# Token factor of a norm as a ScalarE step, norm weights folded into the gate and value rows, and a new hand-written order for the first stage

## The chip, the cores and the metric

One Trainium2 chip, one core of it. The metric is the device time of one execution in microseconds (us). The engines that appear below are TensorE (PE in the rows; its weight loads are PEld), VectorE (DVE), ScalarE (ACT), GpSimd (POOL) and SyncE (SP), which here issues the DMA transfers. Each engine runs its own instructions in the order of the program and waits at the first one whose inputs or buffers are not ready.

## What is computed

Attention in chunks of 64 tokens, an RMS norm with a weight per column, a gated layer, and a second layer with a cosine gate:

```python
scores = scale * np.matmul(q_c, k_c.transpose(0, 1, 2, 4, 3))
scores = scores - np.max(scores, axis=-1, keepdims=True)
attn = np.exp(scores)
attn = attn / (np.sum(attn, axis=-1, keepdims=True) + 1e-09)
out = np.matmul(attn, v_c)
...
rms = np.sqrt(np.mean(x * x, axis=-1, keepdims=True) + 1e-06)
xn = x / rms * rms_g
g = xn @ w_gate
silu = g * (1.0 / (1.0 + np.exp(-g)))
val = xn @ w_val
x = silu * val @ w_out
...
h = x @ w_in
return (h * np.cos(h)) @ w_out2
```

There are 4608 tokens of 512 columns (8 heads of 64), d_ff is 1536 in the first layer and 2048 in the second, all in float32.

## The kernel before

**Stages.** Stage 1 does the attention and the norm of all tokens and, beside them, the first four of the twelve blocks of 128 gate and value columns ("plain" blocks f = 0 to 3). The later stages do the rest of the gate and value columns, and the other three products, by a seven-product scheme on halves of the matrices. Every float32 product is made of three matmuls on high and low parts (`mm3`, L293): high times high, high times low, low times high. The change lies in stage 1, and in weights that stage 1 prepares for the next stage.

**Stage 1.** The tokens are 36 units of 128, taken as 18 pairs, and their products run over chunks of tokens A to K: A to D have 256 tokens, E to K have 512. A step of stage 1 has a letter and a number, and the steps stand in one hand-written list, ORDER (L643 on), which is emitted as it stands; so each engine sees its own instructions in the order of that list. The steps that matter here:

- `Q`, `V`, `D`, `Dg`: loads of queries and keys, of values, of raw plain weights, and of the norm's weights. `Q0` is split in two halves. `Dg` loads `gamma` broadcast to 128x512.
- `s` (and `sx`, the second unit of the first pair): 64x64 score matmuls of a pair on PE (L404), into one PSUM bank for each unit. `m` (L417) row maxima and `b` (L425) subtraction on DVE, `e` (L429) exponential on ACT, `n` (L434 to L436) sum and reciprocal on DVE.
- the product p·z (L444): on GpSimd as a step `z` for units under POOL_Z, on DVE at the end of `n` for the others. `t` (L451) transposes of p on PE, `c` (L456) copy of them on ACT, `v` (L467) the value matmuls of a pair on PE, into `o`.
- the norm: `r` (L481) squares and sums on ACT, `w` (L486, L488) the token factor `rs` on GpSimd, `y` (L492) `xn = o * rs * gamma` on DVE, `x` (L500) transposes on PE into `tr`.
- operands: `j` (L509) cast of `tr` to the high part `xt` and `a` (L514) copy to `xf`, both on ACT; `l` the low part, on GpSimd (L520) for units under POOL_L, on DVE (L522) for the others.
- a plain weight fm (f the block, m = 0 gate, 1 value): `k` (L119, ACT), `p` (L122, L123, DVE) and `q` (L127, L128, DVE) round it, `H` (L544, ACT) casts the high part, `L` (L546, GpSimd) makes the low part.
- the sixteen weights of the later blocks, `P` steps with a number: `Pl` load, `Pa` (L119, ACT), `Pb` (L122, L123, DVE), `Pc` (L127, L128, DVE), `Pd` sums (L198, GpSimd), `Ph` casts (L610, ACT), `Po` low parts (L614, GpSimd), `Pk` store. In the rows they are the tile `wt`.
- `gCf`, `vCf`: the twelve gate or value matmuls of chunk C and block f on PE; `S` (L568) silu on ACT, `h` (L578) product on DVE, `Y` store.

PE runs `gA0` only when `w[0,0]` has its high and low part and the operands of units 0 and 1 stand; in the list the steps `v0`, `v2`, the scores of four pairs, six `t` and four `x` stand ahead of it. The silu of ACT and its exponential use different function tables, so a step `S` after an `e` (or the reverse) is preceded by a table load.

Of the kernel before, what the change touches and what calls it, by code (L numbers as in the profile page):

```python
# [40 lines left out]
POOL_Z = 4  # L41
POOL_L = 4
# [40 lines left out]
def kernel(  # L83
# [26 lines left out]
    def f32(a):  # L110
        return a.bitcast(F32)
# [247 lines left out]
    with ExitStack() as st:  # L359
# [4 lines left out]
        gamma = tp.tile([P, D], F32, tag="gamma", name="gamma")  # L364
# [24 lines left out]
        def part(h):  # L389
            return slice(h * HD, (h + 1) * HD)  # L390
# [4 lines left out]
        def att_s(u, which=(0, 1)):  # L395
            for b in which:
                at = ps_g.tile([P, D], F32, tag="gv", name="sc") if u // 2 in (1, 3) else bank("sc")
                unit[u + b]["sc"] = at.rearrange("p (a b) -> p a b", b=HD)
            for hp in range(NHP):
                for c in range(2):  # L400
                    for b in which:
# [56 lines left out]
        def att_v(u):  # L458
            for b in range(2):
                unit[u + b]["o"] = bank("o")  # L460
            for hp in range(NHP):
                for h in range(2):
                    for b in range(2):
                        s = unit[u + b]
                        for c in range(2):
# [3 lines left out]
                                s["pts"][part(c ^ b), hp, part(h ^ b)],  # L469
# [64 lines left out]
        def conv_step(kind, f, m):  # L534
            if kind == "k":
                conv[f, m] = wp.tile([P, D], U32, tag=f"p{8 + (2 * f + m) % 7}", name="t")
# [49 lines left out]
        def prep_step(kind, j):  # L586
# [34 lines left out]
        units.update({"s": lambda u: att_s(2 * u, (0, 1) if u else (0,)), "z": unit_z, "v": lambda u: att_v(2 * u), "W": lambda k: free(f"p{k}")})  # L621
        units["O"] = lambda j: (hig(0, j), log(0, j))

        def step(name):
            kind, n = name[0], name[1:]
            if name == "Dg":
                nc.sync.dma_start(out=gamma, in_=rms_g[None, :].to_broadcast([P, D]))
            elif name == "sx":
                att_s(0, (1,))
# [14 lines left out]
            Q0 s0 I m0 Q1 b0 sx Q2 e0 m1 Q3 b1 e1 V0 n0 D21 D20 z0 s1 n1 z1 t0 k21 m2 m3 b2 b3 p21 t1 c0 V1 Pl0 e2 c1 e3 n2  # L644
            z2 k20 Dg v0 r0 Q4 n3 q21 w0 p20 Pa0 r1 t2 w1 y0 z3 x0 Q5 c2 t3 H21 a0 j0 Pb0 y1 x1 V2 V3 D00 s2 q20 Q6 D01 c3
            j1 a1 H20 Pc0 m4 m5 b4 v1 b5 e4 r2 e5 L20 l1 r3 n4 n5 Q7 V4 t4 t5 w2 k01 w3 l0 V5 c4 y2 Pl1 k00 D10 p00 y3 x2 c5
            s3 q00 a2 j2 p01 x3 H00 a3 v2 m6 L21 q01 l2 L00 b6 X0 D11 r5 r4 m7 gA2 w4 y4 H01 gA0 vA2 b7 L01 k10 j3 e6 n6 Q8
            V6 x4 vA0 V7 Q9 Pl2 SA2 l3 w5 SA0 t6 e7 p10 hA2 y5 D30 Q10 n7 gB2 x5 D31 Q11 a4 j4 c6 a5 l4 j5 gB0 t7 c7 V8 l5
            hA0 s4 v3 SB2 k11 m8 q10 X1 Pa1 Pd0 m9 b8 H10 vB2 r6 SB0 vB0 w6 V9 r7 w7 hB2 hB0 p11 b9 y6 L10 gC0 gC2 x6 e8 q11
            vC2 e9 gC1 SC0 SC2 n8 vC0 y7 n9 k31 j6 gA1 hC2 H11 Ph0 L11 t9 Po0 hC0 l6 t8 k30 a6 SA1 s5 p30 YA2 Q12 c9 Q13 q30  # L650
            m10 YB2 SC1 x7 a7 p31 b10 YB0 YC0 V10 j7 c8 H30 q31 m11 vC1 YA0 e10 YC2 vA1 hC1 L30 b11 v4 gB1 hA1 l7 r9 e11 X2
            w9 SB1 r8 w8 n10 X3 n11 y8 gB3 H31 gA3 y9 t10 V11 vB1 YC1 SB3 Pa2 L31 t11 s6 Pb2 Pb1 m12 hB1 c10 SA3 vA3 b12 m13
            vB3 Pk0 c11 x8 e12 hA3 b13 x9 e13 v5 j8 a8 Pc1 n12 hB3 a9 gD1 r10 r11 j9 l8 n13 Pd1 w10 l9 V12 Q14 Q15 V13 gD0
            w11 vD1 gD3 t13 y11 YA3 SD1 c13 hD1 y10 t12 s7 x10 Pc2 c12 vD0 m15 m14 Q16 Ph1 Pl3 V14 x11 Po1 j10 SD0 gC3 V15
            Q17 SD3 a10 b14 l10 b15 e14 e15 hD0 j11 v6 r13 a11 SC3 r12 Pa3 w13 Pd2 YB1 Q18 w12 n15 l11 n14 vD3 vC3 Pk1 y13
            YA1 Ph2 hC3 t15 gD2 V16 X4 Pl4 y12 t14 vD2 c14 Po2 s8 Pb3 hD3 c15 x12 SD2 V17 Q19 j12 Pa4 a12 m16 b16 hD2 m17
# [677 lines left out]
```

## Time and profile before

| | us |
|---|---|
| median of 3 runs | 1636.64 |
| lowest, highest | 1635.1, 1636.64 |
| profiled execution, its own time | 1635.3 |
| its span | 1633.5 |
| PE busy in the span | 1604.3 (98%) |
| DVE, ACT, POOL busy in the span | 1378.7, 959.5, 243.2 |

The profile is of one execution. A window's row gives the busy time of each engine in a stretch; a timeline lists instructions with their start and length, runs of like ones on one line; a waits view names for an engine what ended each of its waits; the chain is the work that ended last, followed back from the end; lines by form group equal instructions and give the mean of one in ns.

### The profile page before, as it was taken

How to read it: one execution, taken by the hardware profiler on the slowest of the kernel's cores; microseconds unless marked ns; L12 is line 12 of the kernel's file. 1: busy time of each engine (PE TensorE's matmuls, PEld its weight loads, DVE VectorE, ACT ScalarE, POOL GpSimd, SP SyncE). 2: the span in 40 equal slices, each digit the busy share in tenths (PEclk: the TensorE clock that was granted, in tenths of full speed). 3: DMA queues.
4: the chain of work that ended last, by engine and by line, in shares of the span. 5: the costliest groups of instructions: out<-in, count | busy, mean ns of one | idle time of the engine just before them, and what ended most of it. 6: DMA issues, size and time to landing. Idle time of an engine off the chain costs nothing.

```text
span 1633.5 us, 29216 instructions
## 1 busy us (share of the span) xinstructions
PE 1604.3 (98%) x11208; PEld 1556.4 (95%) x11208; DVE 1378.7 (84%) x1854; ACT 959.5 (59%) x1380; POOL 243.2 (15%) x280
## 2 busy tenths in 40 slices
PE   5999999999999999999999999999999999999998
PEld 4988888999999999999999999999999999999998
DVE  7988785589998997899999788988989977877885
ACT  4877665344555654455554578888888644434443
POOL 4434353023322222001112000000000000000000
PEclk7999999999999999999999999999999999999999
DMA  9588987898678679877576974434433665346331
GB/s 316 198 264 287 302 267 253 288 309 275 200 241 263 219 217 294 322 235 226 187 227 216 335 264 136 155 121 141 138 124 119 235 211 160 101 126 184 108 100 35
DMA packets 293531, 342.98 MB, mean 210 GB/s; under 512 B 87952, under 2 KB 266128, under 8 KB 293392
## 3 DMA queue, kind: packets, MB, share of 16 engines
q1 hardware_dynamic: 292592, 341.02, 64.4%
q8 instruction: 88, 1.44, 0.3%
q14 instruction: 51, 0.42, 0.1%
q10 hardware_dynamic: 800, 0.10, 0.0%
HBM read 197.92 MB, written 143.13 MB: 209 GB/s over the span
## 4 chain that ended last, share of the span: by engine, by line
PE 88%; DVE 6%; DMA 3%; issue 1%; ACT 1%; SPq 1%; POOL 0%; DVEq 0%; ACTq 0%; POOLq 0%
PE b L293 74%; PE v L293 6%; PE g L293 5%; DMA kout<-wout 1%; PE sc L404 1%; PE tr L500 1%; PE o L467 1%; DMA qk<-in_qk_dram 1%; PE pt L451 1%; DVE z L793 0%; DMA w<-kgv 0%; DVE z L782 0%; DVE xo L840 0%; DVE wraw L198 0%; DVE wt L127 0%
## 5 line engine op out<-in xcount | busy, mean ns | idle before, releaser
L293 PE MATMUL b<-xo,w 128*128 128x384 f32 x3528 | 613.0, 334 | 0.3 <-DVE xo L840 0.3
L293 PEld LDWEIGHTS b<-xo,w 128*128 128x128 f32 x3528 | 611.4, 188 | 1.6 <-ACT xo L280 0.7
L293 PE MATMUL b<-xt,w 128*128 128x384 f32 x1728 | 305.2, 335 | 2.3 <-ACT z L778 1.4
L293 PEld LDWEIGHTS b<-xt,w 128*128 128x128 f32 x1728 | 299.6, 188 | 4.5 <-ACT z L778 2.9
L293 PE MATMUL b<-x,w 128*128 128x384 f32 x1440 | 262.3, 335 | 1.4 <-DVE z L782 1.4
L293 PEld LDWEIGHTS b<-x,w 128*128 128x128 f32 x1440 | 250.1, 188 | 3.1 <-DVE z L782 2.0
L280 ACT CAST xo<-q 128x768 fp32r<-128x768 f32 x144 | 118.3, 836 | 117.6 <-PE b L293 97.7
L281 DVE TENSOR_TENSOR xo<-q,xo 128x768 fp32r<-128x768 f32 x144 | 135.3, 954 | 53.2 <-ACT xo L280 53.0
L293 PE MATMUL b<-q,w 128*128 128x384 f32 x864 | 158.0, 334 | 0.0
L293 PEld LDWEIGHTS b<-q,w 128*128 128x128 f32 x864 | 150.5, 188 | 0.2 <-DVE q L945 0.2
L835 ACT CAST xo<-rawh 128x768 fp32r<-128x768 f32 x98 | 80.0, 836 | 62.3 <-PE b L293 41.4
L251 POOL TENSOR_TENSOR wout<-wt,wout 128x384 fp32r<-128x384 f32 x44 | 51.4, 1169 | 424.9 <-ACT wout L249 329.5
L778 ACT COPY z<-b 128x768 f32<-128x768 f32 x72 | 57.6, 800 | 86.7 <-PE b L293 66.1
L293 PE MATMUL v<-xt,w 128*128 128x512 f32 (+1 forms) x528 | 108.2, 356 | 0.0
L293 PE MATMUL g<-xt,w 128*128 128x512 f32 (+1 forms) x528 | 107.6, 356 | 0.0
L840 DVE TENSOR_TENSOR xo<-rawh,xo 128x768 fp32r<-128x768 f32 x98 | 96.9, 1021 | 7.1 <-ACT xo L835 7.0
L293 PEld LDWEIGHTS g<-xt,w 128*128 128x128 f32 x528 | 85.4, 189 | 13.2
L293 PEld LDWEIGHTS v<-xt,w 128*128 128x128 f32 x528 | 85.4, 189 | 12.9
L782 DVE TENSOR_TENSOR z<-b,z 128x768 f32<-128x768 f32 x72 | 68.6, 953 | 29.8 <-PE b L293 22.2
L923 DVE TENSOR_TENSOR u<-b,z 128x768 f32<-128x768 f32 x72 | 68.6, 953 | 17.1 <-ACT z L918 14.0
L251 POOL TENSOR_TENSOR wout<-wraw,wout 128x512 fp32r<-128x512 f32 x44 | 69.5, 1581 | 71.3 <-ACT wout L249 67.0
L943 DVE SCALAR_TENSOR_TENSOR q<-q,u 128x768 f32<-128x768 f32 x72 | 68.5, 953 | 12.1 <-ACT q L941 11.7
(134 smaller groups left out, 2099.8 us busy)
## 6 DMA issues: line engine op xcount, KB each, us to landing
wraw<-in_w_dram SPq DMA_DIRECT2D x240, 128.0 KB, 3.6
gd<-q SPq DMA_DIRECT2D x80, 384.0 KB, 2.5
q<-gd SPq DMA_DIRECT2D x80, 384.0 KB, 4.0
rawh<-hd SPq DMA_DIRECT2D x66, 384.0 KB, 4.8
w<-kout SPq DMA_DIRECT2D x49, 512.0 KB, 6.3
qk<-in_qk_dram SPq DMA_DIRECT2D x35, 512.0 KB, 6.1
kgv<-wout SPq DMA_DIRECT2D x16, 896.0 KB, 5.9
w<-kgv SPq DMA_DIRECT2D x28, 512.0 KB, 6.3
```

Of the source, the lines that this page charges most:

```text
L251: nc.gpsimd.tensor_tensor(b[n][:, :, 1], a, f32(b[n][:, :, 0]), op=ALU.subtract)
L280: nc.scalar.copy(hi, a)
L281: nc.vector.tensor_tensor(lo, a, f32(hi), op=ALU.subtract)
L293: nc.tensor.matmul(acc, a, b, start=first and k == 0 and q == 0, stop=k == n - 1 and q == 2, skip_group_check=True)
L404: nc.tensor.matmul(sc[part(h ^ b), 2 * hp + (c ^ b), :], t[part(h), 0, hp, part(c)], t[part(h), 1, hp, part(c)], start=True, stop=True,)
L451: nc.tensor.transpose(s["pt"][:, hp, :], p[:, 2 * hp : 2 * hp + 2, :].rearrange("p a b -> p (a b)"), ident)
L778: nc.scalar.copy(sums[s, g, k], z[s, g, "b1"])
L782: nc.vector.tensor_tensor(t, z[s, g, "b2" if k == 0 else "b5"], t, op=ALU.add)
L835: nc.scalar.copy(to[0], source2(s, g, j))
L840: nc.vector.tensor_tensor(to[1], source2(s, g, j), f32(to[0]), op=ALU.subtract)
L923: nc.vector.tensor_tensor(t, acc, part, op=ALU.add)
L943: nc.vector.scalar_tensor_tensor(q, q, -PI2, u, op0=ALU.add, op1=ALU.mult)
```

## The change

- `gamma` is loaded as 128x4 (column block d in column d), no longer broadcast to 128x512.
- The norm's weights go into the rows of the gate and value weights, on ACT: step `H` scales four 128x128 column blocks of the rounded plain weight before its cast (32 small instructions in all), and a new step `Pg` scales a prepared weight of the later blocks in two 128x256 instructions (32 in all).
- `y` becomes an ACT instruction, `xn = o * rs`, in place of the DVE instruction with `gamma`.
- POOL_Z and POOL_L go from 4 to 2: p·z and the low part of units 2 and 3 move from GpSimd to DVE.
- `Q0` is one load, and the scores of units 0 and 1 share two banks, each unit half of both; their `m` and `b` become two instructions of half the width each.
- ORDER is written anew.

```diff
-POOL_Z = 4
-POOL_L = 4
+POOL_Z = 2
+POOL_L = 2
...
-        gamma = tp.tile([P, D], F32, tag="gamma", name="gamma")
+        gamma = tp.tile([P, ND], F32, tag="gamma", name="gamma")
...
-            step = NHP if n else NHP // 2
-            for k in range(0, NHP, step):
-                nc.sync.dma_start(out=t[:, :, k : k + step], in_=qk[n][:, :, k : k + step])
+            nc.sync.dma_start(out=t, in_=qk[n])
...
+        def first_s(b):
+            if b == 0:
+                pair["s"] = [bank("sc").rearrange("p (u a d) -> p u a d", u=2, d=HD) for _ in range(2)]
+            t, sc = unit[b].pop("qk"), pair["s"]
+            unit[b]["sc"] = sc
+            for hp in range(NHP):
+                for c in range(2):
+                    for h in range(2):
+                        nc.tensor.matmul(
+                            sc[c ^ b][part(h ^ c ^ b), b, hp, :],
...
+            if n < 2:
+                for k in range(2):
+                    nc.vector.tensor_reduce(s["mx"][:, 4 * k : 4 * k + 4], s["sc"][k][:, n], axis=AX.X, op=ALU.max)
...
+                for k in range(2):
+                    m = mx[:, 4 * k : 4 * k + 4].unsqueeze(2).to_broadcast([P, 4, HD])
+                    nc.vector.tensor_tensor(p[:, :, k], sc[k][:, n], m, op=ALU.subtract)
+                return
...
-            nc.vector.scalar_tensor_tensor(s["xn"], s.pop("o"), s.pop("rs"), gamma, op0=ALU.mult, op1=ALU.mult)
+            nc.scalar.activation(s["xn"], s.pop("o"), AF.Copy, scale=s.pop("rs"))
...
-                nc.scalar.copy(w[f, m][:, 0], f32(conv[f, m]))
+                t = f32(conv[f, m])
+                for d in range(ND):
+                    k = slice(d * P, (d + 1) * P)
+                    nc.scalar.activation(t[:, k], t[:, k], AF.Copy, scale=gamma[:, d : d + 1])
+                nc.scalar.copy(w[f, m][:, 0], t)
...
+            elif kind == "g":
+                e = key[1] % 2
+                nc.scalar.activation(t[:, 1:3], t[:, 1:3], AF.Copy, scale=gamma[:, e + 2 : e + 3])
+                nc.scalar.activation(t[:, ::3], t[:, ::3], AF.Copy, scale=gamma[:, e : e + 1])
...
-                nc.sync.dma_start(out=gamma, in_=rms_g[None, :].to_broadcast([P, D]))
+                nc.sync.dma_start(out=gamma, in_=rms_g.rearrange("(d p) -> p d", p=P))
...
         ORDER = """
-            Q0 s0 I m0 Q1 b0 sx Q2 e0 m1 Q3 b1 e1 V0 n0 D21 D20 z0 s1 n1 z1 t0 k21 m2 m3 b2 b3 p21 t1 c0 V1 Pl0 e2 c1 e3 n2
+            Q0 s0 I Q1 m0 b0 Q2 sx m1 e0 b1 e1 Q3 n0 Pl0 s1 n1 Pa0 Dg Pb0 z0 m2 V0 Pc0 m3 V1 t0 z1 c0 t1 Pl1 D01 c1 Pg0 Q4
```

What the new list does to the engines is shown at three places. In the rows of the order, `sc` are scores, `mx` their maxima, `p` the exponentials, `z` the reciprocal sums, `t` a plain weight while it is rounded, `wt` a weight of the later blocks, `xn` the normed tokens, `xf` and `xt` the operands, `w` a finished plain weight.

PE, the first scores, before and after: what each run of matmuls waits for stands in brackets.

```order
L404 MATMUL sc<-qk 64x64 [waits DMAHW0_49]
L404 MATMUL sc<-qk 64x64 x7
L404 MATMUL sc<-qk 64x64 [waits DMAHW1_49]
L404 MATMUL sc<-qk 64x64 x7
L404 MATMUL sc<-qk 64x64 [waits DMAHW2_49]
L404 MATMUL sc<-qk 64x64 x15
```

```order
L401 MATMUL sc<-qk 64x64 [waits DMAHW0_49]
L401 MATMUL sc<-qk 64x64 x15
L401 MATMUL sc<-qk 64x64 [waits DMAHW1_49,DVE_49]
L401 MATMUL sc<-qk 64x64 x15
L418 MATMUL sc<-qk 64x64 [waits DMAHW2_49]
```

The first unit's sixteen matmuls now follow one transfer instead of two, and the second unit's wait for DVE (the reads of the shared banks by unit 0) beside their transfer.

DVE, right behind the two reciprocals of units 0 and 1, before and after:

```order
L417 TENSOR_REDUCE mx<-sc 128x8 x2
L425 TENSOR_TENSOR p<-sc,mx 128x512 x2
L122 TENSOR_SCALAR t<-t 128x512
L123 TENSOR_SCALAR t<-t 128x512
L434 TENSOR_REDUCE z<-p 128x8
L435 TENSOR_SCALAR z<-z 128x8
L436 RECIPROCAL z<-z 128x8
L434 TENSOR_REDUCE z<-p 128x8
```

```order
L122 TENSOR_SCALAR wt<-wt 128x512
L123 TENSOR_SCALAR wt<-wt 128x512
L435 TENSOR_REDUCE mx<-sc 128x8
L127 SCALAR_TENSOR_TENSOR wt<-wraw,wt 128x512
L128 SCALAR_TENSOR_TENSOR wt<-wraw,wt 128x512
L435 TENSOR_REDUCE mx<-sc 128x8
L450 TENSOR_TENSOR p<-sc,mx 128x512 x2
L459 TENSOR_REDUCE z<-p 128x8
L460 TENSOR_SCALAR z<-z 128x8
L461 RECIPROCAL z<-z 128x8
L469 TENSOR_TENSOR p<-p,z 128x512
```

The first weight of the later blocks is now rounded here (`Pb0`, `Pc0`), and p·z of units 2 and 3 follows their reciprocals on DVE.

ACT, around the cast `H00` that `gA0` needs, before and after:

```order
L119 ACTIVATE t<-raw 128x512
L456 COPY pts<-pt 128x512
L514 COPY xf<-tr 128x4x128
L509 CAST xt<-tr 128x4x128
L544 CAST w<-t 128x512
L514 COPY xf<-tr 128x4x128
L481 ACTIVATE xn,ss<-o 128x512 x2
```

```order
L119 ACTIVATE t<-raw 128x512
L517 ACTIVATE xn<-o,rs 128x512
L481 COPY pts<-pt 128x512
L517 ACTIVATE xn<-o,rs 128x512
L573 ACTIVATE t<-t,gamma 128x128 x4
L574 CAST w<-t 128x512
L534 CAST xt<-tr 128x4x128
L539 COPY xf<-tr 128x4x128
```

The cast now follows two norm steps and four scalings.

## Rows read from the trace of the kernel before

**Rows 1.** Windows: start:end, length, busy us (instructions) by engine, clock, DMA share, GB/s.

```profile
0.00:41.81 41.81, 23.61 (x488) 19.44 (x488) 32.27 (x56) 19.05 (x36) 17.67 (x26) 0.80 0.97 318
...
13.84:37.80 23.96, 14.42 (x292) 11.59 (x290) 23.18 (x44) 14.63 (x30) 13.35 (x16) 0.68 1.03 336
...
37.80:78.81 41.01, 39.09 (x592) 37.39 (x584) 38.30 (x70) 32.58 (x59) 18.28 (x23) 0.98 0.60 202
...
38.51:85.40 46.89, 44.69 (x686) 42.60 (x685) 44.01 (x82) 34.90 (x65) 20.08 (x26) 0.99 0.64 216
...
100.00:150.00 50.00, 49.38 (x673) 41.91 (x674) 42.06 (x79) 38.01 (x70) 24.42 (x40) 1.00 0.90 285
```

**Rows 2.** Waits of PE from 0 to 42 us: total us, times, longest.

```profile
PE sc L404 <- DMA qk<-in_qk_dram: 6.3, 4, 3.9
PE pt L451 <- DVE p L444: 5.6, 2, 3.7
...
PE o L467 <- issue: 1.2, 1, 1.2
```

**Rows 3.** Waits of PE from 42 to 310 us.

```profile
PE pt L451 <- DVE p L444: 1.2, 3, 0.6
PE sc L404 <- ACT xf L514: 0.5, 1, 0.5
PE sc L404 <- DVE xn L492: 0.3, 1, 0.3
```

**Rows 4.** Timeline of PE: start us, length us, instruction, tile, shapes, count.

```profile
41.81 3.14 PE L293 MATMUL g<-xt,w 128*128 128x256 f32 x24
...
88.08 3.14 PE L293 MATMUL g<-xt,w 128*128 128x256 f32 x24
```

**Rows 5.** Chain that ended last, between 80 and 100 us: start us, length us, what.

```profile
86.18 0.87 PE tr L500 x8
87.05 1.09 PE o L467 x64
...
92.65 1.44 PE g L293 x12
```

**Rows 6.** Timeline of DVE, single instructions.

```profile
6.88 0.69 DVE L417 TENSOR_REDUCE mx<-sc 128x8 f32<-128x512 f32 x1 [6.88 <-PE sc L404]
...
37.72 1.50 DVE L122 TENSOR_SCALAR t<-t 128x512 f32<-128x512 f32 x1
39.25 1.38 DVE L123 TENSOR_SCALAR t<-t 128x512 uint32<-128x512 uint32 x1
...
76.97 0.67 DVE L434 TENSOR_REDUCE z<-p 128x8 f32<-128x512 f32 x1
```

**Rows 7.** Timeline of POOL: the low part of the first gate weight.

```profile
38.89 1.45 POOL L546 TENSOR_TENSOR w<-t,w 128x512 fp32r<-128x512 f32 x1
```

**Rows 8.** Lines by form, 0 to 330 us: count, busy us, mean ns, idle before.

```profile
L492 DVE SCALAR_TENSOR_TENSOR xn<-o,rs,gamma 128x512 f32<-128x512 f32 x36 | 26.6, 745 | 8.0 <-POOL rs L488 8.0
L444 DVE TENSOR_TENSOR p<-p,z 128x512 f32<-128x512 f32 x32 | 25.5, 797 | 1.1
...
L522 DVE TENSOR_TENSOR xt<-tr,xt 128x512 fp32r<-128x512 f32 x32 | 21.6, 684 | 10.6 <-ACT xt L509 6.0 <-ACT xf L514 4.7
...
L127 DVE SCALAR_TENSOR_TENSOR wt<-wraw,wt 128x512 uint32<-128x512 uint32 x18 | 12.9, 719 | 0.2
L123 DVE TENSOR_SCALAR wt<-wt 128x512 uint32<-128x512 uint32 x18 | 12.2, 676 | 0.6
...
L122 DVE TENSOR_SCALAR wt<-wt 128x512 f32<-128x512 f32 x18 | 8.8, 486 | 1.4 <-ACT wt L119 1.4
...
L481 ACT ACTIVATE xn<-o 128x512 f32<-128x512 f32 x36 | 21.4, 598 | 15.4 <-PE o L467 15.4
...
L429 ACT ACT_TABLE_LOAD x16 | 20.5, 1283 | 1.0 <-PEq L1320 0.7
...
L568 ACT ACTIVATE sg<-g 128x256 f32<-128x256 f32 x16 | 5.9, 389 | 3.7 <-DVE h L578 3.6
```

More of the change, by code (lines that the diff above doesn't have):

```diff
@@ L393, in bank, with att_s @@
             return ps_at.tile([P, D], F32, tag="at", name=name)
-        def att_s(u, which=(0, 1)):
-            for b in which:
+        def first_s(b):
[8 more added lines that the diff above has]
+                            sc[c ^ b][part(h ^ c ^ b), b, hp, :],
+                            t[part(h), 0, hp, part(c)],
+                            t[part(h), 1, hp, part(c)],
+                            start=True,
+                            stop=True,
+                        )
+        def att_s(u):
+            for b in range(2):
                 at = ps_g.tile([P, D], F32, tag="gv", name="sc") if u // 2 in (1, 3) else bank("sc")
@@ L400, in att_s @@
                 for c in range(2):
-                    for b in which:
+                    for b in range(2):
                         t, sc = unit[u + b]["qk"], unit[u + b]["sc"]
@@ L410, in att_s @@
                             )
-            for b in which:
+            for b in range(2):
                 unit[u + b].pop("qk")
@@ L468, in att_v @@
                                 s["o"][part(c), col],
-                                s["pts"][part(c ^ b), hp, part(h ^ b)],
+                                s["pts"][part(c ^ b), hp, part(h ^ b ^ (0 if u else c))],
                                 s["v"][part(c ^ b), col],
@@ L535, in conv_step @@
             if kind == "k":
-                conv[f, m] = wp.tile([P, D], U32, tag=f"p{8 + (2 * f + m) % 7}", name="t")
+                pair["k"] = pair.get("k", -1) + 1
+                conv[f, m] = wp.tile([P, D], U32, tag=f"p{8 + pair['k'] % 7}", name="t")
                 convert0(raw1[f, m], conv[f, m])
@@ L620 @@
         units.update({"Q": load_qk, "V": load_v, "X": store_x})
-        units.update({"s": lambda u: att_s(2 * u, (0, 1) if u else (0,)), "z": unit_z, "v": lambda u: att_v(2 * u), "W": lambda k: free(f"p{k}")})
+        units.update({"s": lambda u: att_s(2 * u) if u else first_s(0), "z": unit_z, "v": lambda u: att_v(2 * u), "W": lambda k: free(f"p{k}")})
         units["O"] = lambda j: (hig(0, j), log(0, j))
@@ L626, in step @@
             if name == "Dg":
-                nc.sync.dma_start(out=gamma, in_=rms_g[None, :].to_broadcast([P, D]))
+                nc.sync.dma_start(out=gamma, in_=rms_g.rearrange("(d p) -> p d", p=P))
             elif name == "sx":
-                att_s(0, (1,))
+                first_s(1)
             elif name == "I":
@@ L643 @@
         ORDER = """
-            Q0 s0 I m0 Q1 b0 sx Q2 e0 m1 Q3 b1 e1 V0 n0 D21 D20 z0 s1 n1 z1 t0 k21 m2 m3 b2 b3 p21 t1 c0 V1 Pl0 e2 c1 e3 n2
-            z2 k20 Dg v0 r0 Q4 n3 q21 w0 p20 Pa0 r1 t2 w1 y0 z3 x0 Q5 c2 t3 H21 a0 j0 Pb0 y1 x1 V2 V3 D00 s2 q20 Q6 D01 c3
-            j1 a1 H20 Pc0 m4 m5 b4 v1 b5 e4 r2 e5 L20 l1 r3 n4 n5 Q7 V4 t4 t5 w2 k01 w3 l0 V5 c4 y2 Pl1 k00 D10 p00 y3 x2 c5
-            s3 q00 a2 j2 p01 x3 H00 a3 v2 m6 L21 q01 l2 L00 b6 X0 D11 r5 r4 m7 gA2 w4 y4 H01 gA0 vA2 b7 L01 k10 j3 e6 n6 Q8
@@ L648 @@
[L648 to L656, printed above, removed]
@@ L676 @@
-            YI1 Po15 x33 v17 Pk15 j32 SJ3 l32 r34 vJ2 w34 vJ0 y34 YD3 hJ2 a32 r35 j33 x34 SJ0 gJ1 l33 hJ3 w35 y35 YD1 a33
-            X16 j34 x35 SJ1 j35 l35 l34 vJ1 hJ0 W19 a34 gK2 gK0 W20 W21 a35 X17 Z W15 W16 hJ1 vK2 SK2 SK0 hK2 vK0 gK3 W17
-            W18 YJ3 hK0 SK3 gK1 O1 SK1 vK3 O2 vK1 hK1 hK3 YJ1 YK3 YK1
+            Q0 s0 I Q1 m0 b0 Q2 sx m1 e0 b1 e1 Q3 n0 Pl0 s1 n1 Pa0 Dg Pb0 z0 m2 V0 Pc0 m3 V1 t0 z1 c0 t1 Pl1 D01 c1 Pg0 Q4
+            b2 V2 v0 e2 b3 e3 r0 Pd0 r1 Q5 D20 V3 w0 y0 n2 Pa1 Q6 t2 n3 Pb1 x0 k01 p01 D00 Pc1 q01 t3 D31 c2 w1 y1 s2 m4 m5
@@ new lines @@
+            a0 j0 Ph0 k20 b4 c3 p20 x1 Q7 D21 b5 H01 q20 v1 a1 j1 e4 e5 n5 t5 D10 V4 l0 Po0 V5 r2 r3 Q8 n4 t4 k31 H20 k00 c5
+            k21 p00 w3 w2 y3 s3 q00 c4 l1 L01 y2 m6 m7 b6 H00 x2 x3 j2 a2 X0 Pl2 L00 L20 j3 l2 v2 gA0 r5 b7 D11 l3 r4 e6 p21
+            n6 gB0 e7 k10 q21 SA0 vA0 n7 p10 V6 Q9 t6 w4 y4 a3 vB0 w5 V7 H21 y5 SB0 gB2 x4 x5 c6 V8 D30 Q10 j4 hB0 a4 hA0
+            L21 SB2 q10 l4 p31 j5 gA2 Q11 a5 H10 l5 vB2 t7 s4 c7 q31 Pg1 k11 Q12 V9 Pk0 gC0 m8 hB2 SA2 v3 k30 H31 SC0 p11
+            vA2 L10 Pd1 YB0 m9 b8 b9 X2 V10 r7 vC0 Pa2 q11 gA1 gC2 r6 hA2 e8 p30 YA2 hC0 e9 H11 gB1 w6 vC2 n8 w7 X1 Q13 YA0
@@ new lines @@
+            n9 q30 Pb2 YB2 t8 y6 y7 V11 t9 s5 SA1 c8 YC0 m10 L11 c9 SC2 x6 L31 Ph1 H30 hC2 j6 b10 m11 vA1 b11 hA1 Pc2 vB1 x7
+            Pl3 SB1 e11 v4 L30 Pl4 gC1 r8 j7 r9 gB3 a6 e10 l6 n11 a7 hB1 l7 w8 n10 w9 y8 y9 vC1 gA3 SC1 hC1 t11 Q14 t10 SB3
+            Po1 Pa4 s6 c10 c11 m13 m12 YB1 vB3 SA3 Pg2 b12 vA3 x9 b13 YA1 hA3 x8 e12 Pd2 j8 a8 v5 hB3 Q15 n12 l8 Pb4 r11 YC2
+            YA3 r10 Pk1 gC3 V12 V13 e13 w11 a9 j9 l9 V14 n13 X3 Q16 gD1 vC3 t12 vD1 Ph2 y11 w10 Pc4 y10 Po2 SC3 t13 s7 gD3
@@ new lines @@
+            j30 Pa15 a30 SI3 Pd14 m34 l30 j31 b34 v16 m35 l31 gJ2 r33 b35 Pb15 Pc15 w33 V34 Ph14 Pg15 a31 X15 hI1 V35 gJ3
+            hI3 r32 e34 gJ0 y33 e35 SJ2 Po14 w32 n34 YI1 Pk14 t34 vJ2 Pd15 YI3 SJ0 W20 W21 n35 t35 hJ2 y32 c34 Ph15 x32 j32
+            c35 x33 j33 SJ3 a32 vJ0 Po15 v17 r34 r35 l32 w34 a33 X16 w35 l33 hJ0 gJ1 vJ3 y34 y35 x34 SJ1 j34 l34 x35 j35
+            Pk15 a34 vJ1 hJ3 l35 hJ1 gK2 gK0 a35 X17 Z W15 W16 YJ3 SK2 SK0 gK3 vK2 gK1 W17 W18 vK0 O1 hK2 hK0 SK3 vK3 O2 SK1
+            hK3 vK1 hK1 YK1 YJ1 YK3
```

45 lines of the change are left out of this document (25 added, 20 removed).

## The prediction

> **What bounds the kernel now.** I read the busy shares first: TensorE is busy for 98% of the span, and the tenths show its only thin slice at the very start. So a gain must come from the first microseconds, where TensorE has too little to do, or from its later waits. The waits name the latter: from 42 us to the end of the stage TensorE waits 1.2 + 0.5 + 0.3 = 2.0 us [rows 3]. Work that leaves VectorE there can give back 2.0 us at most.
>
> To measure the start I count what TensorE owes: the time at which a product starts, less the work that stands ahead of it in the list. The prices are 1.09 us for 64 small matmuls (value products, and the same for scores of a pair), 0.87 for eight 128-column transposes, and 1.44 for twelve matmuls of a group [rows 5]. Ahead of the first group `gA0` stand four pairs of scores, three of values and ten transposes: 7 x 1.09 + 10 x 0.435 = 12.0 us. It starts at 41.81 [rows 4], so 29.8 us are lost by then. Ahead of `gD1`, at 88.08 [rows 4], stand seven pairs of scores, six of values, 22 transposes and 22 groups: 13 x 1.09 + 22 x 0.435 + 22 x 1.44 = 55.4, so 32.7 us are lost. The debt grows by only 2.9 us between, and then hardly at all. The time of the kernel is this debt plus work that does not change; what I have to find is the debt after the change.
>
> What makes it: up to 41.81 the transfers take 97% of the DMA time and the mean clock is 0.80 [rows 1]; TensorE waits 6.3 us for the first queries and keys, and 5.6 us for p·z from VectorE [rows 2]. From 13.84, where the reciprocals of unit 1 end, to 37.80, where the first gate weight is rounded (`q00`), VectorE is busy 23.18 of 23.96 us, and from there to the end of p·z of unit 10 at 78.81 it is busy 38.30 of 41.01 [rows 1]. So VectorE's row of work from unit 1 to about `gD1` sets the debt. Only later, at 42.06 of 50 us [rows 1], does it have slack.
>
> **The change part by part.** Seen by totals, 36 norm steps of 745 ns leave VectorE [rows 8], 26.6 us. Of these only those ahead of about 80 us count, and the list puts other work there.
>
> *First load and shared banks.* Before, maxima of unit 0 start at 6.88 [rows 6]. One transfer in place of two should start unit 0's scores later and finish them sooner. I take the end of its maxima and subtraction at 7.6, and unit 1's scores must now wait for that, since VectorE still reads the banks. With two half-width instructions in place of one for `m` and `b`, at about 0.1 us more each, I come to 12.8 us for the end of unit 1's reciprocals, against 13.84: a head start of 1.0 us. It lies between 0 (the wait takes all back) and 1.6.
>
> *VectorE from unit 1 to `q00`.* Added: p·z of units 2 and 3, 2 x 0.797 = 1.59; rounding of one more weight of the later blocks, 0.486 + 0.676 + 2 x 0.719 = 2.60. Removed: four norm steps, 4 x 0.745 = 2.98 [rows 8]. Two further roundings are exchanged for two others. Net +1.2 us, and about 0.7 for `Pb1`, which stands in front of the queue while ScalarE still has `Pa1` to do: 12.8 + 23.96 + 1.2 + 0.7 = 38.7, against 37.80. What is queued behind `Pb1` on VectorE is all the rest up to `q00`.
>
> *From `q00` to `gA0`.* The cast `H00` gets four scalings of 128 columns. No row shows one. The nearest is the 128x256 silu at 389 ns [rows 8]: half of it, 0.19, is the lower end, and 0.48, that row and a tenth, the upper; I take 0.30, nearer to the half, as the columns are half. That is 1.2 us on the path, then the cast at about 0.5 and the low part on GpSimd at 1.45 [rows 7]. 38.7 + 1.2 + 0.5 + 1.4 = 41.8. Before, the low part ended at 40.34 [rows 7], and TensorE still stood in the values of units 4 and 5, with a wait of 1.2 us marked "issue" [rows 2]. That slack swallows the difference: `gA0` starts at about 41.8 in both kernels, and the debt there is again 29.8.
>
> *VectorE from `q00` to p·z of unit 10.* Added: one more reciprocal and p·z, 78.81 - 76.97 = 1.84 [rows 1, 6]; the low parts of units 2 and 3, 2 x 0.684 = 1.37; another rounding, 2.60. Removed: four norm steps, 2.98 [rows 8]. Net +2.8; some of these means hold stretches in which VectorE stood beside GpSimd (see the first rival), so I take +2.6. Then p·z of unit 10 ends at 38.7 + 41.0 + 2.6 = 82.3. TensorE has 11 x 1.09 + 19 x 0.435 + 20 x 1.44 = 49.1 us of work ahead of the transposes of unit 10 in the new list, so the debt is 33.2, against 32.7 at `gD1` before: +0.5.
>
> *Afterwards.* VectorE is relieved of a norm step in each unit, and nothing is added but a rounding here and there. The 2.0 us of TensorE's waits [rows 3] lie mostly behind 88 us; with VectorE ahead I take back half, 1.0. Sum: +0.5 - 1.0 = -0.5 us.
>
> *ScalarE.* It gets 36 norm steps at 0.598 for the same tile (the row of the squares [rows 8]; 0.5 if they overlap as those do, 0.75 if the factor operand costs as much as on VectorE), 32 small scalings at 0.30, 32 of 256 columns at 0.42 (the 389 ns row and a little), less two table loads of 1.283: 21.5 + 9.6 + 13.4 - 2.6 = 42 us in about 268, of which about 9 fall between 42 and 100. From the end of `H00` to the copy of unit 11, which the values `v5` need, it was busy 34.90 of 46.89 us [rows 1]; to this come six norm steps, twenty small scalings and two larger, less two table loads: 3.6 + 6.0 + 0.8 - 2.6 = 7.8. Half of its idle time would be left, so I cost it at nothing; the second rival says what it costs otherwise. The factor `rs` comes from GpSimd, and its 8.0 us of idle time [rows 8] move from VectorE to ScalarE, ahead of the copies and exponentials queued there.
>
> *Smaller parts, at nothing:* the load of `gamma` is 128 rows of four separate numbers and is first needed by the scaling behind `Pc0`; the scalings of the later weights stand between VectorE and sums on GpSimd that no product in this stage needs.
>
> ScalarE's move is one that a page warns of. The trace shows 598 ns on ScalarE and 745 on VectorE for a 128x512 instruction that reads `o` [rows 8]. The Trainium skill, "ScalarE: Activation LUTs", section "Rules for kernel authors", says to multiply on VectorE and not on ScalarE; by that rule the second rival would be the likely one. For fp32 and this tile the trace disagrees.
>
> **Forecast and rivals.** The profiled execution took 1635.3 us against a median of 1636.64; by the sum it becomes 1634.8, and I add half of the 1.3 between the two: **1635.5 us**, chance 0.44, its own range 1633.4 to 1638.
>
> *Rival 1, VectorE comes through the start sooner: 1632.0 us, chance 0.32.* Before, just behind `q00`, a TENSOR_SCALAR takes 1.50 and 1.38 us [rows 6] while GpSimd makes a low part from 38.89 on [rows 7], against a mean of 0.486 and 0.676 for the same pair [rows 8]: 1.7 us lost at one place. GpSimd now has two p·z and two low parts less. If 2.7 us of such blocking fall out before `q00`, it ends at 36, `gA0` starts at 39.1 (if the loads of values stand by then), and with the debt near 29.5 the kernel gains 4: 1635.3 - 4 + 0.7 = 1632.0. Against it: the sums of a prepared weight come early to GpSimd, and the transfers were at 97% in that stretch, so values may not land sooner. The Trainium skill, "SBUF — State Buffer", section "SBUF: two separate sides", has VectorE and GpSimd take one pair of ports as a lock, for whole instructions, where VectorE has two inputs in SBUF or a fast mode; the 1.50 agrees. By it p·z, with both inputs in SBUF, brings back on VectorE some of what leaves GpSimd.
>
> *Rival 2, ScalarE becomes the last: 1640.7 us, chance 0.18.* `H00` ends at about 40.4; 34.9 + 7.8 = 42.7 us of work bring ScalarE to the copy of unit 11 at 83.1 plus whatever it idles. `v5` has 54.3 us of TensorE work ahead and would be due at 54.3 + 32.7 = 87.0. So it decides from 4 us of idle time on. Before, ScalarE idled 46.89 - 34.90 = 12.0 us there; if 8.6 remain (in-order waits for `rs`, for transposes, for VectorE), `v5` comes 4.7 us late: 1635.3 + 4.7 + 0.7 = 1640.7. For it: a norm step now stands ahead of the transposes of each unit, behind a wait for GpSimd, and 8.0 us of such waits were seen. Against it: much of the idle time was waiting for VectorE, which is now ahead.
>
> *Rival 3, the start doesn't move as it should: within 1 us of the median, chance 0.06.* If unit 1's scores wait for all of unit 0's subtraction, or the four-byte rows of `gamma` land after 16 us, the head start is gone and `q00` ends 1 us later; the slack of 1.2 us ahead of `gA0` hides most of it: 1636.5.
>
> About 0.2%, 3.3 us, is what a measurement of this kernel can tell from no change. Faster by more than that holds nearly all of rival 1 and a little of the forecast's lower end: 0.34. Slower holds most of rival 2 and a little of the upper end: 0.18. Between: 0.48. For the range I reach over the whole of rival 1 and to the middle of rival 2: 1631.0 to 1640.5, which leaves one in ten at each end.
>
> **What would show it.** In the profile of the changed kernel: the reciprocals of unit 1 end at 12.8; `q00` at 38.7 (at 36 if rival 1 holds); the first group starts at 41.8 (39.1); p·z of unit 10 ends at 82.3; a small scaling takes 0.19 to 0.48; TensorE waits under 1 us from 100 to 310. Rival 2 shows as waits of the transposes `tr` or the values `o` for ScalarE, with ScalarE busy over 90% from 42 to 100. The forecast is wrong if the first group moves by more than 2 us either way, or if the debt grows between it and 120 us by other than 3 to 4.

## The result: slower by 11.5 us, and where it shows

| | before | after |
|---|---|---|
| median of 5 runs, us | 1636.64 | 1648.09 |
| lowest, highest | 1635.1, 1637.63 | 1647.09, 1649.81 |
| span of the profiled execution | 1633.5 | 1646.9 |
| ACT busy | 959.5 | 999.7 |
| DVE busy | 1378.7 | 1354.7 |

The ratio is 1.0072 (95% interval 1.0062 to 1.0083). The forecast was no change. Work did move from VectorE to ScalarE, near the totals of the prediction: ScalarE is busy 40 us more (42 forecast), VectorE 24 us less (26.6 forecast). The question is what TensorE waited for.

The waits of TensorE after 42 us, in the changed kernel; [rows 3] had 2.0 us in all:

```profile
PE pt L476 <- DVE p L469: 4.5, 5, 2.0
PE g L293 <- DVE xt L547: 3.6, 1, 3.6
PE g L293 <- DVE h L608: 1.5, 1, 1.5
PE tr L525 <- ACT pts L481: 1.2, 1, 1.2
PE g L293 <- ACT sg L598: 0.5, 1, 0.5
PE sc L418 <- ACT xn L517: 0.2, 1, 0.2
PE g L293 <- POOL w L576: 0.2, 1, 0.2
```

They sum to 11.7, which is 9.7 more; 4.2 of the 11.7 lie before 100 us and 7.5 behind it. The longest, 3.6 us for one low part `xt`, costs more than itself. The timeline of TensorE around it, and the windows of that stretch (columns as in [rows 1]):

```profile
240.45 5.06 PE L293 MATMUL g<-xt,w 128*128 128x512 f32 x11 [3.62 <-DVE xt L547]
...
245.91 2.99 PE L293 MATMUL g<-xt,w 128*128 128x512 f32 x12
```

```profile
236.80:240.45 3.65, 0.03 (x1) 0.00 (x0) 0.74 (x2) 3.62 (x7) 3.49 (x6) 0.80 0.69 196
240.45:246.00 5.55, 5.55 (x16) 4.38 (x17) 5.27 (x12) 0.37 (x1) 0.56 (x2) 0.52 1.00 312
```

Eleven matmuls take 5.06 us behind the stall, where twelve take 2.99 right after. The granted clock is 0.52 in that stretch, about the lower level of 1.2 GHz, and 1.00 again from 246 us on. At 2.99 for twelve, eleven would be 2.74, so the slow stretch costs 2.3 us. 9.7 + 2.3 = 12.0 us, near the 11.5 of the medians and the 13.4 of the spans.

The slow stretch doesn't follow every stall. In `no_scalings` (below) TensorE stands 2.8 us at the same place, and behind it eleven matmuls take 2.79 us at a granted clock of 1.00:

```profile
238.24 2.79 PE L293 MATMUL g<-xt,w 128*128 128x512 f32 x11 [2.82 <-DVE xt L547]
```

The same stall on the other engines (timelines of ScalarE and of VectorE):

```profile
229.85 0.59 ACT L534 CAST xt<-tr 128x512 fp32r<-128x512 f32 x1 [0.98 <-PE tr L525]
233.81 0.60 ACT L506 ACTIVATE xn<-o 128x512 f32<-128x512 f32 x1 [3.38 <-PE o L492]
...
235.90 0.58 ACT L539 COPY xf<-tr 128x512 f32<-128x512 f32 x1
236.37 0.53 ACT L636 ACTIVATE wt<-wt,gamma 128x256 f32<-128x256 f32 x1
236.78 0.51 ACT L637 ACTIVATE wt<-wt,gamma 128x256 f32<-128x256 f32 x1
237.31 1.28 ACT L598 ACT_TABLE_LOAD   x1
238.60 0.60 ACT L598 ACTIVATE sg<-g 128x512 f32<-128x512 f32 x1
239.09 0.58 ACT L539 COPY xf<-tr 128x512 f32<-128x512 f32 x1
```

```profile
239.71 0.69 DVE L547 TENSOR_TENSOR xt<-tr,xt 128x512 fp32r<-128x512 f32 x1 [7.08 <-ACT xf L539]
```

This low part is `l27`, tr minus the high part. Its high part stands at 230.44 (first row). It starts at 239.71, right behind the end of `a27`, the copy of the same `tr` to `xf`, at 239.67, although it uses nothing of `xf`. In the compiled program this subtraction does wait for ScalarE's count at the copy: where `a` stands ahead of `l` in the list, the second reader of the PSUM tile is made to wait for the first. `a27` stood four steps ahead of `l27`; on ScalarE two squares, of which the first waited 3.4 us for its values, two casts, a copy, two scalings, a table load and a silu stood ahead of it.

In the windows (ScalarE is the fifth figure, 19.75 of 20 us in the first) ScalarE is full early on and not later:

```profile
40.00:60.00 20.00, 19.80 (x321) 18.60 (x320) 18.38 (x33) 19.75 (x47) 9.56 (x12) 0.98 0.46 142
60.00:80.00 20.00, 18.04 (x260) 17.36 (x259) 17.35 (x32) 19.25 (x42) 8.42 (x12) 1.00 0.71 223
...
200.00:250.00 50.00, 44.55 (x481) 35.77 (x483) 30.07 (x54) 34.32 (x64) 18.35 (x31) 0.93 0.85 264
```

### The profile page after: what moved, and what is told of

The parts are those of the page before. It is cut to its first block, busy times and chain, and to the rows that moved or that the text cites. A ratio compares the mean times of both kernels' runs of the same rounds, so it can differ in the third digit from the quotient of the medians.

```text
span 1646.9 us, 29275 instructions
## 1 busy us (share of the span) xinstructions
PE 1607.9 (98%) x11208; PEld 1558.3 (95%) x11208; DVE 1354.7 (82%) x1826; ACT 999.7 (61%) x1478; POOL 236.0 (14%) x276
## 4 chain that ended last, share of the span: by engine, by line
PE 85%; DVE 8%; ACT 3%; DMA 2%; issue 2%; SPq 0%; POOL 0%; DVEq 0%; ACTq 0%; POOLq 0%
PE b L293 74%; PE v L293 4%; PE g L293 4%; DMA raw<-in_w_dram 1%; PE o L492 1%; PE pt L476 1%; PE tr L525 1%; PE sc L418 1%; DVE wraw L198 1%; DVE xo L875 1%; DVE p L469 1%; DVE z L459 0%; DMA xd<-xf 0%; DMA kgv<-wout 0%; DVE z L828 0%
```

## Experiments

Two theories stood against each other. **Load:** ScalarE has 40 us more to do, and TensorE waits for that. **Order:** single steps stand at places in the list where an engine's queue holds them back, and the same instructions in other places would not cost it. All times below are medians; the kernel before ran beside each, at 1636.3, 1636.7, 1636.0 and 1635.8 in the four sets. The intervals are some 1.5 to 2 us to either side, so a difference of about 1 us between two runs isn't clear of the noise.

**One copy moved.**

```diff
-w28 a27 Pl13 YH3 Q34 l27 n31
+w28 Pl13 YH3 Q34 l27 a27 n31
```

> The changed kernel with one step of the list moved: the copy a27 stands behind the low part l27 instead of 4 steps ahead of it, so that l27 on VectorE no longer waits for that copy on ScalarE. Order theory: the stall of 3.6 us ahead of the group gI2 and the 2.2 us that the matmuls behind it lose at a lower granted clock go, 1642 to 1643.5. Load theory: ScalarE is late anyway, the next step that hangs on it waits instead, and under 2 us come back, 1646 to 1648.

1642.97 (1.0038, 1.0025 to 1.0051): one step moved by four places gives 5.1 us back. VectorE's timeline of this kernel has the low part right behind the rounding of a weight, and TensorE runs through, with the group `gI2` at full clock:

```profile
233.13 0.69 DVE L547 TENSOR_TENSOR xt<-tr,xt 128x512 fp32r<-128x512 f32 x1
```

```profile
237.03 2.89 PE L293 MATMUL g<-xt,w 128*128 128x512 f32 x12
```

**y back to VectorE, with the new list.**

```diff
-nc.scalar.activation(s["xn"], s.pop("o"), AF.Copy, scale=s.pop("rs"))
+nc.vector.tensor_scalar(s["xn"], s.pop("o"), s.pop("rs"), None, op0=ALU.mult)
```

> The changed kernel with the norm step y on VectorE again (o times the token factor, no norm weights in it); order, scalings and everything else as in the changed kernel. Load theory (TensorE waits because ScalarE has too much to do): 36 steps of 0.58 us, 21 us, leave ScalarE, so most of the 11.5 us come back, 1638 to 1640, and the wait of 2.0 us at 68 us for p*z shrinks. Order theory (the stalls come from where the list puts single steps in an engine's queue): under 4 us come back, 1644 to 1648, and the stall of 3.6 us at 237 us stays.

1662.22 (1.0153, 1.0139 to 1.0167). Both were wrong: taking 20 us off ScalarE (979.7 busy for 999.7) makes it 14 us slower. In the waits of TensorE up to 42 us and in VectorE's timeline:

```profile
PE pt L476 <- DVE p L469: 8.9, 3, 5.0
PE tr L525 <- DVE xn L517: 4.8, 1, 4.8
```

```profile
19.63 0.75 DVE L517 TENSOR_SCALAR xn<-o,rs 128x512 f32<-128x512 f32 x1 [2.19 <-POOL rs L513]
```

The new list has `y0` in a place where the token factor isn't there yet; VectorE's whole row stands 2.2 us behind it, four such steps add 3.0 us to that row, and the first group starts at 48.7 instead of 42.1. That is 6.7 of the 14 us; behind the first group TensorE's waits sum to 15.1 instead of 11.7, and the granted clock is 0.93 from 48.7 to 100 us, where it was 1.00 from 42 on. The place of `y0` as the cause is read from the trace; no run moved it. The list was made for y on ScalarE. On VectorE the step takes 745 ns, with or without `gamma` [rows 8]; on ScalarE it takes 698. The Trainium skill, "ScalarE: Activation LUTs", section "Rules for kernel authors", would have multiplications on VectorE. The rows of the single instruction don't bear that out for this fp32 tile in PSUM. The times go both ways: here VectorE is 14 us worse, and in the old list, below, it is 2.1 us better (1636.72 against 1638.83).

**The old arithmetic in the new list** (y with `gamma` on VectorE, no scalings).

> The changed kernel with its new order, first load, shared banks and GpSimd shares, but the old arithmetic: weights of the norm broadcast to 128x512, y on VectorE with them, no scalings. Load theory: ScalarE is back at its old load, 1636 to 1640. Order theory: 1643 to 1648.

1658.23 (1.0129, 1.0115 to 1.0143), slower than both of its parents. The trace has the same wait of `y0` (2.19 us at 19.60), and the first group starts at 47.8. **The new arithmetic in the old list** (scalings inserted as steps Pg, each right behind its Pc):

```diff
-Pc1 ... Pd1
+Pc1 Pg1 ... Pd1
```

> The kernel before with its own order, but with the new arithmetic: norm weights 128x4, four scalings ahead of each cast H, two scalings behind each Pc, the norm step y on ScalarE. First load, banks and the GpSimd shares stay as before. Load theory: ScalarE has the same 42 us more, so 1644 to 1650. Order theory: the old list holds, 1636 to 1640.

1655.12 (1.0113, 1.0099 to 1.0127). Neither half does well with the other's list, so a swap of whole lists can't tell load from order. So the arithmetic was split, in the old list.

**Only y on ScalarE** (the norm's weights left out), and **only the scalings** (y on VectorE):

> The kernel before with its own order, in which only the norm step y goes to ScalarE (o times the token factor; the norm's weights are left out of the computation, no scalings). ScalarE gets 21 us, VectorE loses 27. Load theory: about half of the 18.8 us that old_order lost, 1643 to 1647. Order theory: the old list puts y where VectorE had room and ScalarE has not, in front of the transposes; it carries most of the loss, 1647 to 1653.

> The kernel before with its own order, y on VectorE as o times the token factor, and the 64 scalings of weights on ScalarE. Load theory: the other half, 1643 to 1647. Order theory: a scaling stands ahead of a cast or of sums on GpSimd which no product waits for soon, but in the first 42 us four of them stand on the way to the first group: 1637 to 1642.

1638.83 (1.0014, 1.0005 to 1.0022) and 1648.36 (1.0069, 1.0056 to 1.0083). The order theory had it upside down: 36 steps of ScalarE that stand ahead of the transposes cost 2 us, and the 64 scalings, which I had taken to be far from any product, cost 11.6. Neither theory's range holds either time. Alone the two cost 13.7 us, together 18.8 (`old_order`), so 5 us come only with both. The groups of `old_scalings` and its waits of ScalarE say why:

```profile
L610 ACT ACTIVATE wt<-wt,gamma 128x256 f32<-128x256 f32 x16 | 8.2, 511 | 27.0 <-DVE wt L128 27.0
```

```profile
ACT wt L610 <- DVE wt L128: 27.0, 11, 7.9
```

Right behind Pc in the list, the scaling waits in ScalarE's queue for VectorE to reach that rounding, up to 7.9 us at once and 27 in all, with exponentials, copies and silus behind it. In the changed kernel, whose list has Pg later, the same wait is 4.4 us. By the traces the loss is that wait rather than 26 us of scalings; no run takes the wait away alone, so it is argued.

**Pg moved to right ahead of the sums Pd**, otherwise as `old_order`:

> As old_order (the order of before, all of the new arithmetic), but each pair of scalings of a later weight stands right ahead of its sums Pd instead of right behind its rounding Pc. Same instructions, same load. Order theory: ScalarE waits less for VectorE's rounding in front of its own queue, 20 us before, under 10 now, and 4 to 9 of the 18.8 us come back: 1646 to 1651. Load theory: no change, 1653 to 1656.

1663.80 (1.0169, 1.0155 to 1.0183), 9 us slower still, by neither theory. ScalarE's wait for the rounding falls from 20.0 us in `old_order` to 2.5, but a wait of GpSimd for the scalings, 36.4 there, rises to 61.2 (waits of GpSimd, 42 to 310 us):

```profile
POOL wsum L198 <- ACT wt L611: 61.2, 12, 10.1
```

```profile
L492 ACT ACTIVATE xn<-o,rs 128x512 f32<-128x512 f32 x36 | 24.5, 692 | 12.2 <-POOL rs L488 12.2
```

The sums now wait on GpSimd, the token factors `rs` are queued behind them there, and y on ScalarE waits 12.2 us for `rs` (8.1 in `old_order`), with TensorE's transposes behind it. In these traces the wait went round by a third engine.

**The scalings taken out of the changed kernel** (norm's weights left out), without and with the copy moved:

> The changed kernel without the 64 scalings of weights on ScalarE (the norm's weights are left out of the computation); y stays on ScalarE, order unchanged. ScalarE has 23 us less. Load theory: the waits of TensorE at 68 and 82 us and most of the loss go, 1638 to 1642. Order theory: the stall of 3.6 us ahead of gI2 and the slow matmuls behind it stay (a copy that stands ahead of a low part is no scaling), 1643 to 1647.

> The changed kernel with a27 behind l27 and without the 64 scalings (norm's weights left out of the computation). If the place of the copy and the load of the scalings cost separately, 5.1 and 4.3 us less than the changed kernel, minus about 1 that both hold at 237 us: 1639 to 1640.5. If it is all one cause: 1642 to 1643.5.

1643.76 (1.0042, 1.0029 to 1.0054) and 1639.52 (1.0021, 1.0013 to 1.0030). 21.5 us less on ScalarE give 4.3, and the stall at 237 us stays in the first:

```profile
PE g L293 <- DVE xt L547: 3.3, 2, 2.8
```

Together they give 8.6 of the 9.4 that the single ones (5.1 and 4.3) add up to. So they add up but for 0.9 us, which is within the noise. In the traces they do meet at the stall: without the scalings it is 2.8 us instead of 3.6, and no slow stretch follows it.

**Nine steps moved, and four copies moved.** `tuned` moves a27, a25, a6, a7 behind their low parts and five other steps; `four_copies` only the copies:

```diff
-gB3 a6 e10 l6 n11 a7 hB1 l7 w8
+gB3 e10 l6 a6 n11 hB1 l7 a7 w8
...
-Pa12 a25 gH0 w27 y27 l25 n28
+Pa12 gH0 w27 y27 l25 a25 n28
...
-w28 a27 Pl13 YH3 Q34 l27 n31
+w28 Pl13 YH3 Q34 l27 a27 n31
```

> The changed kernel with the same instructions and nine steps of the list moved: copies a27, a25, a6, a7 behind the low parts of their units; c30 ahead of the silu SI2; Pa2 behind e9; q11, H11 and p30 behind n9. Order theory: beyond the 5 us of a27 alone, the waits at 220 us (1.5), 82 us (1.4 and 0.3) and 264 us (1.1) go, and half of the 2.0 at 68 us with the slow stretch behind it: 1636 to 1639. Load theory: ScalarE has the same work, so the waits reappear a few steps later: 1641 to 1643.

> The changed kernel with four copies moved and nothing else: a27, a25, a6, a7 each right behind the low part of its unit. Order theory: beside the 5 us of a27, the waits of 1.5 us at 220 and of 1.4 + 0.3 us at 84 go: 1639 to 1641. If ScalarE's load is what is left, they come back elsewhere: 1642 to 1643.5.

1642.27 (1.0034, 1.0021 to 1.0046) for nine and 1639.83 (1.0021, 1.0012 to 1.0030) for four. The four give back 8.3 of 11.5 us. 1642.27 lies in the load theory's range, but it is the five others that cost 2.4. In the trace, with q11 and H11 behind n9 ScalarE waits at H11 for VectorE, y6 and y7 stand behind it, and the scores of pair 5 wait for them (waits of ScalarE, and of TensorE from 62 to 80 us, in `tuned`):

```profile
ACT t L573 <- DVE t L128: 3.9, 1, 3.9
```

```profile
PE sc L418 <- ACT xn L517: 3.2, 2, 2.9
```

**What is left.** In `four_copies` TensorE still waits 4.6 us after 42, and 2.0 of it for p·z of unit 9:

```profile
PE pt L476 <- DVE p L469: 3.0, 4, 2.0
PE tr L525 <- ACT pts L481: 1.1, 1, 1.1
PE g L293 <- ACT sg L598: 0.5, 1, 0.5
```

> four_copies without the 64 scalings (the norm's weights are left out of the computation). If what four_copies still loses is the load of the scalings on ScalarE: 1635.5 to 1637.5. If it is VectorE's row at the start, which they are no part of: 1638.5 to 1640.

> four_copies, and the second weight of the later blocks (Pa1 to Pk1) is rounded, scaled and summed behind p*z of unit 10 instead of ahead of the first group; the steps of weights 2 and 4 that would collide with it in buffers stand a little later. Same instructions. If VectorE's row up to q00 and to p*z of units 9 and 10 holds the rest of the loss (the new list put two more weights into it than the old one), 2.6 us leave it: the first group starts at 39.5 to 40.5 instead of 42.15, the wait of 2.0 us at 68 goes, 1635 to 1637.5. If it is ScalarE's load or the transfers, 1639 to 1640.5.

1636.48 (1.0001, 0.9993 to 1.0010) without the scalings, so the remaining 3.4 us go with them: the first p·z wait above falls to 0.9. Between them the four copies and the scalings account for all of the 11.5 us. Both theories were right in part: the order of the copies is 8.3 us, the scalings 3.4.

Most of the 2.0 us at 68 us can be seen in VectorE's timeline of `four_copies`. A step that takes 0.17 us elsewhere takes 0.74, and p·z takes 1.47 instead of 0.69, together 1.35 us more, while GpSimd makes two low parts (last row below, 66.60 to 69.10):

```profile
67.17 0.74 DVE L460 TENSOR_SCALAR z<-z 128x8 f32<-128x8 f32 x1
...
68.18 1.47 DVE L469 TENSOR_TENSOR p<-p,z 128x512 f32<-128x512 f32 x1
```

```profile
66.60 2.50 POOL L576 TENSOR_TENSOR w<-t,w 128x512 fp32r<-128x512 f32 x2 [1.47 <-DVE p L469]
```

In `four_no_scalings` GpSimd makes them from 64.32 on, and the slow p·z is that of the other unit of the pair (1.49 us at 65.92), which nothing waits for. So part of what is left is the blocking beside GpSimd that the prediction's first rival names; two traces show it together in time, and no run isolates it.

Taking a weight's rounding out of VectorE's row ahead of the first group (`late_weight`) gives 1638.74 (1.0013, 1.0004 to 1.0022), 1.1 us only, which isn't clear of the noise. The first group does start earlier:

```profile
39.25 0.50 PE L293 MATMUL g<-xt,w 128*128 128x256 f32 x2
```

That is 2.9 us earlier than in `four_copies`, about as expected, but TensorE then waits 1.8 us for p·z near 68 and 1.7 near 85: most of a gain at the first group is given back at the next units.

**The first load alone, in the kernel before** (whole Q0, shared banks; nothing else of the change), and the same with the first later weight rounded behind n10:

> The kernel before with only the first load whole and the scores of units 0 and 1 in two shared banks. The reciprocals of unit 1 should end at 12.2 us as in the changed kernel, against 13.84, and the first group start up to 1.6 us earlier: 1634.5 to 1636.5. If the loads hold the first group (wait marked issue), it stays at 41.5 to 41.9 and the time within 0.5 us of before.

> before_first (the kernel before with the whole first load and the two shared banks), and the first weight of the later blocks is loaded behind the second's old place and rounded behind p*z of unit 10. VectorE's row theory: 2.6 us less ahead of the first group, which starts at 38.5 to 39.5 instead of 41.15, and less on the transfers there; part is given back by 120 us, where VectorE is full: 1630.5 to 1633. If the transfers or the instruction stream hold the first group: 1633 to 1635.

1633.90 (0.9986, 0.9977 to 0.9995) and 1642.70 (1.0034, 1.0020 to 1.0047). The first load and the shared banks are the one part of the change that pays: 2.1 us (interval 0.8 to 3.8). The reciprocals of unit 1 end at 12.11 and the first group starts at 41.15:

```profile
11.91 0.20 DVE L461 RECIPROCAL z<-z 128x8 f32<-128x8 f32 x1
```

```profile
41.15 3.14 PE L293 MATMUL g<-xt,w 128*128 128x256 f32 x24
```

The later weight made it worse, outside both ranges. In that kernel the load Pl2, whose buffer Pc0 gives free, stands on SyncE 11.6 us waiting for that rounding, with the loads of values, queries and keys behind it (waits of SyncE, 70 to 104 us); and in the chain the weight's sums and a low part on GpSimd stand ahead of a value group:

```profile
SPq L182 <- DVE wt L128: 11.6, 1, 11.6
```

```profile
85.25 1.24 POOL w L571
86.53 4.93 PE v L293 x22
```

`before_first` has the lowest median of all the kernels run, ahead of both the kernel before and the changed one.

## The prediction, point by point

- **The debt at the first group: right, with some luck.** Forecast 41.8, measured 42.06. Behind it, the reciprocals of unit 1 ended at 12.21 (forecast 12.8), so the head start is 1.6 instead of 1.0. The rounding of the first gate weight ended at 39.39 (38.7): VectorE's row took 27.2 instead of 25.9. From there to the group it was 2.7 instead of 3.1. The three errors cancel. Which group it is was misread: the rows of before at 41.81 are `gA2` and `gA0`, in this order; the changed list has `gA0` first. The sum doesn't depend on it. The rows of after that answer to [rows 4] and [rows 6]:

```profile
42.06 0.51 PE L293 MATMUL g<-xt,w 128*128 128x256 f32 x2
```

```profile
12.01 0.20 DVE L461 RECIPROCAL z<-z 128x8 f32<-128x8 f32 x1
...
38.70 0.69 DVE L128 SCALAR_TENSOR_TENSOR t<-raw,t 128x512 uint32<-128x512 uint32 x1
...
84.19 0.69 DVE L469 TENSOR_TENSOR p<-p,z 128x512 f32<-128x512 f32 x1
```

- **The prices: within their bounds.** Four small scalings take 1.28 us together (0.32 each, taken 0.30), one of 256 columns 0.51 alone and 0.41 in a row (taken 0.42), the norm step 0.70 alone (taken 0.60, at most 0.75):

```profile
L517 ACT ACTIVATE xn<-o,rs 128x512 f32<-128x512 f32 x36 | 24.3, 698 | 3.2 <-POOL rs L513 3.2
L573 ACT ACTIVATE t<-t,gamma 128x128 f32<-128x128 f32 x32 | 10.2, 397 | 2.7 <-DVE t L128 2.6
...
L636 ACT ACTIVATE wt<-wt,gamma 128x256 f32<-128x256 f32 x16 | 8.2, 513 | 4.9 <-DVE wt L128 4.4 <-DMA raw<-in_w_dram 0.4
```

  The Trainium skill, "ScalarE: Activation LUTs", section "What ACT_TABLE_LOAD costs", gives 186 ns plus 0.833 per column, and 93 more for a per-partition operand: 386 for 128 columns, an estimate that these 397 bear out.
- **Up to p·z of unit 10: failed by its own sign.** It ended at 84.88, forecast 82.3; with 49.1 us of work ahead, the transposes at 85.02 give a debt of 35.9 instead of 33.2. The debt grew by 5.9 where the prediction had 3 to 4. ScalarE is busy 37.0 of the 38 us from 42 to 80, and 30.4 without the scalings, where the way from the first group to these transposes is 1.2 us shorter. And the low part of unit 6 stood 2.2 us behind the copy `a6`, for which TensorE waited 1.5 us; with the copies moved that wait is gone.
- **"Afterwards": the step that failed.** I took back 1.0 us because VectorE would be ahead. TensorE's waits after 42 us rose from 2.0 to 11.7 instead. From 100 us on, where the debt was to grow by under 1 us, they rose from 0.9 to 7.5, and the slow stretch added 2.3. So some 3 of the 11.5 us were lost by 85 us and 8 to 9 behind it. I had priced the rest of the new list by sums of work, and by sums VectorE and ScalarE both have slack there. The stall at 237 us is on engines that are 60% and 69% busy in their window. What decided, by the four copies (8.3 us), is what stands ahead of what in a queue, and I compared the lists only up to 85 us.
- **"ScalarE ... I cost it at nothing": failed by 3.4 to 4.3 us,** the price of the scalings in the runs. Rival 2 had the engine right and place and mechanism wrong: `v5` never waited for the copy of unit 11; there was no late step that all hung on, but several short waits, some of them behind copies. One of its signs, ScalarE over 90% busy from 42 to 100 us, came close (89%), but the wait that it names, for ScalarE's side of the transposes, came once, 1.2 us.
- **8.0 us of waits for `rs` move to ScalarE: mis-sized.** In the changed kernel they are 3.2 us. The waits that the new steps brought stood elsewhere: 4.4 us of scalings for VectorE's rounding, and a low part held 7.1 us by a copy.
- **Rival 1: not seen at the first group, which would have started at 39.1; seen behind it.** The slow VectorE instructions beside GpSimd are still there, as at 35.98 us, one of 1.49, and such a pair makes most of the 2.0 us wait at 68 us (above). **Rival 3: not seen,** the first load gives 2.1 us where it stands alone.
- **The "issue" wait ahead of the first group: wrongly read as a load of values,** see the last section. As 1.2 us of slack it would have been no better: in the changed kernel no stop stands in the values' row ahead of the first group, which runs through from 40.97 to 42.13.

## What to carry over

In a list that fixes the order on five engines, the cost of a new step is not its length but what it waits for and what stands behind it on its engine; walk each new wait over the whole list, not only up to where the work is tight, and look for pairs of readers of one tile on different engines, since here the second was made to wait for the first. Moved by a few places, one copy gave 5 us and four gave 8; the same idea with a poor place lost as much. A list fitted to one division of work is no test of another, so split the change in the list it was made for, and in both.

## What the runs showed of the hardware beside that

TensorE stops in the middle of a row of 64 small matmuls: 1.2 us before [rows 2], 2.8 in `before_first`, 3.1 in the changed kernel. I had put this to loads of values. The views call all three "issue", a wait for nothing that the profile shows, but they aren't the same. The waits of the changed kernel up to 42 us, and the instructions of that row from 24 to 30 us:

```profile
PE o L492 <- issue: 3.1, 1, 3.1
```

```profile
L492 PEldq EVENT_SEMAPHORE  x2: 51/1696/3340, 24.1 to 25.8; - x2
```

Here a semaphore instruction of 3.34 us stands in the queue of weight loads. In the compiled program it waits for VectorE's subtraction of unit 4, which ends at 29.09; TensorE goes on at 29.19. So "issue" can hide a wait for a semaphore, and the queue's own rows show it. In `before_first` there is no such row at the stop (37.94 to 40.77), only one of 51 ns ahead of it, and in the kernel before none. The transfers from 37 to 38 us in `before_first`:

```profile
q8 instruction: 1, 0.02, 8.5%
```

In these two kernels a 16 KB packet of the instruction queue moves near the start of the stop (39 to 40 us before), while the transfers fill nearly all of the time. That TensorE waits there for its own instructions fits this. But the same packets move at other times too, as at 44 us in both, where the transfers are as dense and TensorE runs through, and no run took the other transfers away, so it is argued and not shown.
